# Down projection of four pairs of token tiles as a Strassen product

## The chip, the cores and the metric

The kernel runs on one core of one Trainium2 chip. The metric is the device time of one execution in microseconds (us). The engines are TensorE (PE, its weight loads are shown as PEld), VectorE (DVE), ScalarE (ACT), GpSimd (POOL) and SyncE (SP), which issues all data transfers (DMAs) here. Each engine works through its own queue in order and waits on semaphores of the others.

## The reference

One transformer block on 2048 tokens of width 512, all in float32: pre-norm sliding-window attention (32 heads of 16, window 256) and then a gated layer.

```python
def _B_ref(x, w_gate, w_up, w_down):
    g = jnp.einsum("bsd,df->bsf", x, w_gate)      # 512 -> 1376
    u = jnp.einsum("bsd,df->bsf", x, w_up)
    h = _sigmoid(g) * u
    return jnp.einsum("bsf,fd->bsd", h, w_down)   # 1376 -> 512

x = A_x
h = x + _A_ref(_layernorm(x, axis=-1), A_wqkv, A_wo)
h2 = h + _B_ref(_layernorm(h, axis=-1), B_w_gate, B_w_up, B_w_down)
```

The change concerns the last product, with `w_down`, for 8 of the 16 tiles of 128 tokens.

## The kernel before

**Numbers.** Every float32 operand of a large product is split into a high and a low float16 half, scaled by a power of two, and a product is three matmuls (high by high, high by low, low by high) that add up in one PSUM accumulator. A matmul has a stationary block of up to 128 x 128 (loaded by a weight load) and streams up to 512 columns past it.

**Stages.** Attention fills the time up to about 400 us. Its blocks overlap: projections (`do_qk`, `do_v`), scores for the row maximum (`do_s`), transposed scores and exponentials (`do_st`), weighted values (`do_pv`), output projection (`do_wo`). From there to about 524 us the weights of the gated layer are loaded, scaled and split (`do_split`, `do_T`), the last attention blocks end, and tiles 0 to 3 go through gate and up projection in the plain way (`do_early`, `do_gu`). The last stage, from about 524 us, takes tiles 4 to 15 in six pairs p = 2 to 7 (tiles 2p and 2p + 1).

**The last stage.** `do_pair` normalizes the two tiles of a pair, forms the Strassen combinations of their activations (S1 to S4), splits them into halves and transposes them by DMA into `x7`. `do_group(p, kind)` then computes gate (kind 0), up (kind 1) and the last 352 columns of both (kind 2) with seven products in place of eight: a pair of tiles and two halves of the contraction make a 2 x 2 matrix, two column blocks of the weight another, and the weight combinations T1 to T4 were made once by `do_T`. Its accumulators X, Y, Z lie in three PSUM banks, from the ring `s`, or from `st` and the bank `pvp`. A first product is copied out (p1), later ones add to it. Group numbers in the table are 3(p - 2) + kind.

The result of kind 1, times the sigmoid of kind 0, gives the hidden activations of 512 columns per tile (columns 0 to 511 and 512 to 1023); kind 2 gives the last 352. `row(t, c, ...)` splits each into halves (`hhi`: a cast on ACT or DVE; `hlo`: a subtraction on DVE or POOL), and a DMA on SP's queue transposes it into a buffer `hT`. `do_down(t)` multiplies: 11 steps over the hidden dimension, each of 3 matmuls with 512 output columns, in one bank of the ring `mm`; then one DVE instruction scales and adds the residual, and a DMA stores the tile:

```python
for f in range(NF):                       # NF = 11
    r = min(P, F - f * P)
    mm3(ps, lambda a, f: hT[t, f // 4][0][:r, a, f % 4, :], lambda a, f: W["d", 3][:r, a, f, :], f, NF)
...
V.scalar_tensor_tensor(y, ps, cd, X[:, slot(t), :], op0=ALU.mult, op1=ALU.add)
```

**Order.** Nothing is scheduled at run time. Each piece (`do_down(4)` and so on) is a generator that yields once per step, with a planned cost per engine, what it needs, and buffers from rings that it takes. A search done beforehand found an order of all steps; it stands in the string `TABLE`, as names such as `down4` or `group3.2/a`. `.2` is the third follow-up piece of group 3; `/a`, `/v`, `/g` choose ACT, DVE or POOL where a step can run on several; `*3` repeats. The steps are emitted in that order, so the table fixes the queue of each engine. A down step of one tile can stand anywhere behind its transposes, and the table puts such steps between the groups' products.

Of the kernel before, what the change touches and what calls it, by code (L numbers as in the profile page):

```python
# [50 lines left out]
SU = float(2.0 ** -16)  # L51
# [25 lines left out]
s2.2 qk8 s2 open_work0 s2 qk8 s2.3 qk8 s2.5 s2.4 ln11 s3 qk8 s3 s2 qk8 s3.0 qk8 s3.1 qk8 ln11 prep3/g prep3/a s2.6 s3 s2 qk9 s3.2 qk8/a amax7/a s3 s2.7 s3.3
qk9 s3*2 qk9 s3.4 s3.5 qk9*2 s4 qk8 s3 qk9*2 s3 qk9 s4.0 s3.6 s4 qk10 s3.7 qk9/a prep3/a amax5/a s4 qk10 s4.1 m0 s4 s4.2 s4 qk10*3 s4 qk10 s4.3 s4.4 s4 m0 qk9
s4.5 m0 s4.6 s5 qk10*2 qk11 s4 qk10/a s5.0 qk11 s5 s4.7 qk11 s5 s5.1 s5.2 s5 qk11 s5.3 s5 qk11*2 s5 s5.4 qk10 qk11 s6 s5.5 s6.0 qk11 s5 s6 s5 qk11/a s5.6 st0
s6.1 st0 ln6 s5.7 s6 st0.0 st0.1 qk11 s6.2 ln7/a s6 st0*2 s6*2 st0.2 ln10 ln8 ln7/g st0.3 st0 keys2 keys1 ln6/a s6.4 s6.3 s6.5 s7 s6 amax8/v keys2 st0 s6 v5  # L80
st0.5 s7.0 s6.6 s6.7 st0.6 s7*2 st1 s7.1 ln7 s7.2 st1.0 st0.4 ln9 st0.7 s7*2 ln7/a ln8/v s7.3 s7.4 st1 s7 s7.5 v5 st1 s7*2 st1.1 st1.2 s7.6 s8 st1 s7.7 st1.3
st1 s8 s8.0 st1.5 s8 st1.4 st1 s8.1 v5 pv0 s8*2 queries8 st1.6 s8.2 m1 queries8 ln8/a st2 s8 s8.3 st1.7 st2 v5 m1 st2.0 s8.4 st2.1 ln8/g s9 st2 s8 s8.5 st2
pv0 v5/a st2.2 ln9/a st2.3 s8.6 s9.0 ln12 ln8 m1 s9 pv0/a s8 st2 st2.5 s9 s9.1 s9.2 keys2 qk14 st2 s9 s8.7 qk14 s9.3 st3 qk14 st2.6 ln12 st2.4 st2.7 pv0 qk14
s9*2 st3 st3.0 st3 s9.4 s9 qk14 st3.1 s9.5 st3.2 qk14 ln9/a s9.6 s9 st3*2 s10 s9.7 st3.3 qk14 s10 ln9/g st3.5 s10.0 st3 s10.1 s10 qk14 st3.6 s10.2 st3.4 st4
s10 qk15 s10 s10.3 st4.0 st4 st3.7 fill1 s11 s10.4 st4 st4.1 pv1 qk15 s11 st4 s10 st4.2 ln10/v qk14/a st4 s10.5 s11.0 s11.1 pv1 queries8 ln9 queries9 o0 amax9
queries9*2 st4.3 st4.5 ln13 st4.4 prep3/g st4 s11 pv1/a s11 st5 st4.6 s11.3 s11.2 qk15 s10 qk15 st5.0 qk15 s10.6 pv1 ln10/a st5*2 s10 s11 qk15 st5.1 o1 st5.2
s10.7 s11 st5 st5.3 st5 s11.4 s11 st5.5 st5 s11.5 pv2 s11 queries10 s11.6 st5.6 ln10/g st4.7 st5.4 qk15*2 st6 s12 s11.7 st6.0 qk14 st5.7 s12 st6 s12 st6 m2
qk15/a pv2 s12.0 s12.2 st6.2 ln11/a st6.1 m2 amax10 amax11 m2 queries10 s12.1 st6 s12*2 pv2/a s12.3 st6 s12 st6.3 st6.5 st6 st6.4 s12.4 s12.5 st6.6 s12 s12.6
st7 s13 st7.0 st7 s12 s13.0 pv2 s12.7 queries10 st7.1 st7*2 s13 st7.2 st7.3 st7 s13 s13.1 s13 st7 st7.5 s13.2 s13 s13.3 queries11 st7.6 st8 s13 s13.4
queries11 st8.0 s13.5 queries11 s13 st8 pv3 s14 s13.6 st8.1 st6.7 o0/g st7.7 st7.4 st8 s13 s14 st8 s14.0 qk15 s14.1 s13.7 ln14 pv3 o2 keys3 st8.3 st8.2 s14  # L90
pv3/a st8*2 s14*2 st8.6 s14.2 qk12*2 st8.7 s14.3 s14.4 st9 s15 o1/g st8.4 st8.5 pv3 s15.0 qk12 st9 s14 st9.0 keys3 o3 st9.1 s15 qk12 st9 s14.5 s14 qk12 st9.2
s15.1 st9 s14 st9.3 s14.6 s15 st9 s15 qk13 s14.7 st9.6 st9.4 st9.5 o2/g st9 s15.2 pv4 s15 qk12 st9.7 s15.3 s15 st10 s15.4 qk13 s15 st10.0 s15.5 s16 qk12 st10
s15.6 st10.1 st9.8 st8.8 s16.0 s16 st10 qk12 s15 s16.1 qk13 s16 st10 st10.2 s15.7 s16 st10 s16 pv4 qk12/a o3/v m3 wo1 s16.4 s16.2 qk12 m3 wo1/g st10.3 st10.6
wo1/a s16.3 wo0 m3 pv4/a st10 s17 st11 s16 s17.0 st10.7 qk13 s16 s16.5 qk13 s16 st11.0 s16.6 st11 s17 s16.7 st11 st11.1 s17 s17.1 wo1/g wo1 ln13 wo0/g st10.5
qk13 st11.2 s17.2 s17 st11 s17 s17.3 qk13 st11.3 s17.4 st11 s17*2 st11.6 st11 s17.5 pv5 s17 qk13 s17.6 st11.7 s18 st12 s17.7 s18.0 s18 st12.0 st12 s18 wo1
s18.1 st11.5 st11.4 st10.4 st10.8 st12.1 st12 s18 st12 s18 s18.2 pv4 st12.2 st11.8 s18 wo1 s18.3 st12.3 s18.4 st12 s18 qk13/a st12.6 st12 st12.7 wo0/a st12.5
s18 st12.8 wo0/g keys2 o4 o4/g ln15 s18.5 s18.6 s18.7 amax9/v pv5 qk13 s19 st13 s19 st13 st13.0 s19.0 s19 wo1 queries12 amax12 queries12 queries13 s19.1
st13.1 s19.2 s19 st13 st12.4 pv5/a s19 s19.3 st13 st13.2 s19.4 s19 wo1 s19.5 pv5 st13.3 s19 st13 qk18 s19 st13.6 st13.5 s19.6 s19.7 st13 st13.7 qk18 s20 st14
m4 s20*2 st14.0 s20.0 st13.8 st14 qk18 s20.2 s20.1 st14.1 s20 st13.4 st14 qk18 st14.2 s20.3 st14 pv6 s20*3 st14 pv6 st14.6 amax10/a st14.3 ln14 amax11/v s20.5
s20.4 s20.6 wo1 amax12/v o5 queries14 wo0 m4 amax15 st14 pv6/a s20 st15 s21 queries13 amax14 queries14 s20.7 amax11 st14.7 s21 wo0 s21.0 st15.0 s21.1 st14.5  # L100
# [187 lines left out]
def tile_block(ctx, tc, x, wqkv, wo, wg, wu, wd, out):  # L288
# [944 lines left out]
    def do_down(t):  # L1233
# [7 lines left out]
        for c in range(3):  # L1241
            plan.free(f"hT{c}", hT[t, c][1], e)
# [216 lines left out]
```

## Time and profile before

| | |
|---|---|
| time, median of 3 runs | 770.11 us (770.04 to 770.41) |
| profiled execution, its own time | 769.71 us |
| span of that execution | 768.0 us |
| instructions in the span | 18055 |
| busy: PE, PEld, DVE, ACT, POOL | 739.6, 466.6, 586.5, 429.5, 339.3 us |
| mean granted TensorE clock | 0.999 |

A span runs from the first to the last instruction; an execution's own time is a little longer. Busy times are of one engine each and overlap one another. A busy PE is not PE at its peak, because consecutive matmuls are drawn overlapping; the distance from one matmul to the next is read from the chain that ended last, which adds up runs of them. A group of instructions is shown with its source line, engine, output and inputs, count, busy time, mean duration of one, and the idle time ahead of it on its engine with what ended it.

### The profile page before, as it was taken

Reading aid. Unit: us, or ns where it says so; the run is one execution under the profiler, and the core shown is the slowest. Engines: PE = TensorE matmul, PEld = TensorE weight load, DVE = VectorE, ACT = ScalarE, POOL = GpSimd, SP = SyncE. Lnnn points to the kernel's source line nnn. Section 1 sums busy time; section 2 is a strip of 40 time slices with the busy share of each in tenths; the row PEclk is TensorE's granted clock in tenths of the full one; section 3 lists DMA queues with packets and bytes.
Section 4 is the critical chain, followed back from the end, with each engine's and each line's share of the span. In section 5 each row is a group of like instructions: output and inputs, shape, how many; then the busy total and the mean of one; then the engine's idle time right before and its main releaser. Section 6 shows DMA issues by size and latency. Waiting matters only on the chain.

```text
span 768.0 us, 18055 instructions
## 1 busy us (share of the span) xinstructions
PE 739.6 (96%) x6714; PEld 466.6 (61%) x6714; DVE 586.5 (76%) x1767; ACT 429.5 (56%) x756; POOL 339.3 (44%) x428
## 2 busy tenths in 40 slices
PE   5799999999999999999999799999999999999998
PEld 4577777777787678787665444454544444444453
DVE  6979999887988888688879989976554657566452
ACT  6736888887776787786778866630142122121220
POOL 8732647554444554555556556430341224234210
PEclk9999999999999999999999999999999999999999
DMA  9883563656946626536455768543434433434333
GB/s 332 216 216 107 146 169 69 164 109 128 198 112 163 136 65 147 105 78 135 85 87 140 181 151 236 124 77 72 99 86 93 107 72 96 83 67 101 66 82 83
DMA packets 168567, 95.68 MB, mean 125 GB/s; under 512 B 140640, under 2 KB 146784, under 8 KB 168480
## 3 DMA queue, kind: packets, MB, share of 16 engines
q1 hardware_dynamic: 168480, 94.54, 52.7%
q8 instruction: 52, 0.85, 0.5%
q14 instruction: 35, 0.29, 0.1%
HBM read 35.26 MB, written 13.11 MB: 63 GB/s over the span
## 4 chain that ended last, share of the span: by engine, by line
PE 79%; DVE 12%; issue 4%; POOL 3%; ACT 2%; DMA 1%; DVEq 0%; POOLq 0%; ACTq 0%
PE mmp L358 31%; PE sp L1086 10%; PE pvp L742 9%; PE sp L654 8%; PE stp L1086 7%; PE stp L716 3%; PE pvp L1086 3%; PE stp L706 3%; PE sp L358 2%; PE stp L705 2%; DVE junk L641 2%; PE stp L707 1%; PE stp L358 1%; DVE Tu L985 1%; ACT pa L683 1%
## 5 line engine op out<-in xcount | busy, mean ns | idle before, releaser
L641 DVE CUSTOM_DVE_ANT_0 junk<-sp,mask 128x320 bf16<-128x320 f32 (+4 forms) x512 | 214.8, 465 | 38.1 <-PE sp L654 35.7
L683 ACT ACTIVATE pa<-stp,kappa 128x512 f32<-128x512 f32 (+1 forms) x256 | 156.0, 645 | 36.5 <-PE stp L707 31.0
L654 PE MATMUL sp<-SK,SQ 96*128 96x256 f16 (+3 forms) x960 | 129.2, 232 | 2.3 <-DVE mq L641 1.6
L1086 PEld LDWEIGHTS <-SQ 128*128 128x128 f16 x756 | 73.9, 98 | 75.5
L358 PE MATMUL mmp<-xT,W 128*128 128x256 f16 x768 | 109.5, 273 | 0.5 <-DVE xT L313 0.5
L358 PE MATMUL mmp<-WD,hT 128*128 128x512 f16 (+1 forms) x408 | 98.7, 379 | 0.0
L654 PEld LDWEIGHTS <-SQ 96*128 96x128 f16 x960 | 79.5, 97 | 26.4 <-issue 9.0
L683 ACT ACTIVATE pb<-stp,kappa 128x512 f32<-128x512 f32 x128 | 84.1, 685 | 19.2 <-PE stp L716 17.2
L689 POOL TENSOR_SCALAR_AFFINE_SELECT pa<-pa 128x1024 f32<-128x1024 f32 x56 | 62.2, 1113 | 38.3 <-ACT pa L683 35.1
L358 PEld LDWEIGHTS <-W 128*128 128x128 f16 x768 | 70.2, 97 | 9.8 <-issue 1.0
L358 PEld LDWEIGHTS <-hT 128*128 128x128 f16 (+1 forms) x408 | 39.9, 98 | 45.3
L694 POOL TENSOR_SCALAR_AFFINE_SELECT pa<-pa 128x512 f32<-128x512 f32 x64 | 41.8, 655 | 53.0 <-ACT pa L683 52.9
L742 PE MATMUL pvp<-pa,VT 128*17 128x128 f32 (+1 forms) x1408 | 62.5, 307 | 0.5 <-DVE rh L754 0.5
L694 POOL TENSOR_SCALAR_AFFINE_SELECT pb<-pb 128x512 f32<-128x512 f32 x64 | 42.0, 660 | 44.0 <-ACT pb L683 43.3
L706 PE MATMUL stp<-SQ,SK 100*128 100x256 f16 x224 | 60.0, 271 | 0.0
L707 PE MATMUL stp<-SQ,SK 100*128 100x128 f16 x256 | 55.3, 218 | 0.5 <-ACT pb L683 0.2
L358 PE MATMUL mmp<-WO,oT 128*128 128x512 f16 x192 | 50.4, 378 | 1.9 <-DMA oT<-whl 1.5
L742 PEld LDWEIGHTS pvp<-pa,VT 128*17 128x17 f32 x1408 | 37.8, 97 | 23.4 <-issue 2.8
L705 PE MATMUL stp<-SQ,SK 100*128 100x128 f16 x224 | 49.4, 220 | 2.7 <-ACT pa L683 1.8
L358 PE MATMUL mmp<-W,xT 128*128 128x512 f16 x192 | 49.7, 378 | 1.9 <-DVE sq L580 1.9
L716 PE MATMUL stp<-SQ,SK 100*128 100x256 f16 x256 | 48.3, 272 | 2.5 <-ACT pa L683 2.4
L358 PEld LDWEIGHTS <-x 128*128 128x128 f16 x288 | 28.0, 98 | 28.5 <-issue 1.8
(322 smaller groups left out, 1351.1 us busy)
## 6 DMA issues: line engine op xcount, KB each, us to landing
SQ<-sq SPq DMA_DIRECT2D x96, 128.0 KB
SK<-mem SPq DMA_DIRECT2D x16, 384.0 KB
chunk<-in_wd_dram SPq DMA_DIRECT2D x20, 256.0 KB
mem<-sk SPq DMA_DIRECT2D x8, 512.0 KB
out_dram<-WO SPq DMA_DIRECT2D x16, 256.0 KB
X<-in_x_dram SPq DMA_DIRECT2D x7, 512.0 KB
chunk<-in_wu_dram SPq DMA_DIRECT2D x12, 256.0 KB
xs<-X SPq DMA_DIRECT2D x10, 256.0 KB
```

The costliest lines, as they stand in the source:

```text
L358: PE.matmul(ps, a_of(a, k), b_of(b, k), start=(k == 0 and i == 0), stop=(k == n - 1 and i == 2))
L641: V.tensor_tensor_reduce(out=junk[:, c0:], in0=ps[:, c0:], in1=mask[:, c0:], scale=1.0, scalar=-3.0e38, op0=ALU.add, op1=ALU.max, accum_ou ...
L654: PE.matmul(ps[:, col:col + k1 - k0], q, SK[0:96, (2 * a + hf) % 5, 4 * (p % 2) + j, k0:k1], start=True, stop=True)
L683: S.activation(dst, a, AF.Exp, scale=kappa)
L689: G.affine_select(out=f, in_=f, pattern=[[0, 8], [-1, 128]], compare_op=ALU.is_gt, fill=0.0, base=0, channel_multiplier=1)
L694: G.affine_select(out=p, in_=p, pattern=[[0, 4], [1, 128]], compare_op=ALU.is_ge, fill=0.0, base=0, channel_multiplier=-1)
L705: PE.matmul(a[:, 0:128], ks(k0, g, j), qs(b, g, j, 0, 128), start=True, stop=True)
L706: PE.matmul(a[:, 128:384], ks(k0 + 1, g, j), qs(b, g, j, 0, 256), start=True, stop=True)
L707: PE.matmul(a[:, 384:512], ks(k0 + 3, g, j), qs(b, g, j, 128, 256), start=True, stop=True)
L716: PE.matmul(a[:, u, :], ks(k0 + 2, g, j + u), qs(b, g, j + u, 0, 256), start=True, stop=True)
L742: PE.matmul(ps[32 * j:32 * j + 17, u, q0:q1], VT[:, kt % 6, 8 * j + g, :], w[:, j, c:c + q1 - q0], start=first, stop=last, skip_group_chec ...
L1086: PE.matmul(out, x7[p][0][:, kk, MATS[a], ha, :], mv, start=first and i == 0, stop=i == 5, skip_group_check=True)
```

## The change

For pairs p = 3 to 6 (tiles 6 to 13) the first 1024 of the 1376 hidden columns of the down projection are multiplied by Strassen's algorithm: the two tiles by two blocks of 512 hidden columns, against two blocks of 512 rows of `w_down` by two blocks of 256 output columns. The other 352 hidden columns are multiplied plainly, in the same accumulators, by output halves of 256 columns (`rest`). Tiles 0 to 5, 14 and 15 keep `do_down`.

- `do_sums(k)`, four times: loads two blocks of `w_down` again, makes T1 to T4 with four subtractions (POOL or DVE), and splits each into halves (a cast and a DVE instruction each). They lie in buffers that other weights have left (`retire`), and the loads use the one buffer `FS`, which `do_pair` also uses from p = 3 on, in place of three.
- `do_mat(p, m)`, seven for a pair: the operands A11, A12, A22 and the sums S1 to S4 of hidden activations, each split into halves and transposed by a DMA. They take the place of four `row` pieces.
- `do_mix(p)`: seven products of 12 matmuls and four remainders of 9, all of 256 columns, with accumulators X, Y, Z in three banks and W in one of `mm`; copies and additions of 256 columns on DVE, ACT or POOL; the residual and the scale are applied by the same DVE instructions that combine; then two stores.
- The rings of row and transpose buffers for the first two column blocks become one each (`h` of 4, `hT` of 6). Scale constants change by powers of two.
- Some planned costs change (for example 0.68 in place of 0.8 for a load of x, 1.1 in place of 0.85 for the rows of maxima), and `TABLE` is found anew from its start: 4458 steps in place of 4345, a different order throughout.

```diff
+MIX = range(3, 7)
...
+                if p in MIX:
+                    Aq[p, "A" + q] = a, i
+                    plan.mark(("a", p, "A" + q), e)
+                    return
                 yield from row(t, c, a, e, lambda z: plan.free("E", i, z))
...
+    def do_sums(k):
+        e, nF = yield {DMA_: 0.475}, ["retired", ("scale", "d")], ["FS"], 0.8
...
+        nc.sync.dma_start(f[:, 0], wd[k * P:k * P + P, :])
...
+        nc.sync.dma_start(f[:, 1], wd[512 + k * P:512 + k * P + P, :])
...
+        e, = yield {POOL_: 2.76, DVE_: 1.4}, [e]
+        E = G if plan.on == POOL_ else V
+        for o, x, y in ((a, b, a), (b, d, b), (d, d, a), (c, c, d)):
+            E.tensor_tensor(out=o, in0=x, in1=y, op=ALU.subtract)
+        for m, x in (("T1", a), ("T3", b), ("T2", d), ("T4", c)):
+            e, = yield {ACT_: 0.4, DVE_: 0.25}, [e]
+            copy(TD[m][:, 0, k // 2, k % 2], x, sc["sd"])
+            e, = yield {DVE_: 0.38}, [e]
+            V.scalar_tensor_tensor(TD[m][:, 1, k // 2, k % 2], x, sc["sd"], TD[m][:, 0, k // 2, k % 2], op0=ALU.mult, op1=ALU.subtract)
...
+    def do_mat(p, m):
...
+        add, sub = {DVE_: 0.602, POOL_: 1.113}, ALU.subtract
+        if m == "S1":
+            e, i = yield add, [("a", p, "A21"), ("a", p, "A22")], ["tp"]
+            x = TP[i % RINGS["tp"]]
+            Hm[p, "M"] = x, i
+            tt(x, quad("A21"), quad("A22"), ALU.add)
...
+        e, nh = yield {ACT_: 0.52, DVE_: 0.335}, [e], ["h"]
+        h = hrow["h"][nh % len(hrow["h"])]
+        copy(h[:, 0], x)
+        e, = yield {DVE_: 0.602, POOL_: 1.113}, [e]
+        subtract(h[:, 1], x, h[:, 0])
...
+        e, nt = yield {DMA_: 1.295}, [e], ["hT"], 1.4
...
+    def do_mix(p):
+        rings, bank = (("s",) * 3, None) if p % 2 else (("st", "st", "pv"), pvp[0])
+        n = D // 2
...
+            for c in range(4):
+                for ha, hb in ((0, 0), (0, 1), (1, 0)):
+                    PE.matmul(ps[r][0], x[:, ha, c, :], moving_d(b, hb, c), start=first and k == 0, stop=last and k == 11, skip_group_check=True)
...
+        e = yield from prod("X", "A11", "B11", True, False, rings[0])
+        plan.add(snap("X", "p1", e))
...
+        e = yield from prod("Z", "S1", "T1", True, False, rings[1])
+        plan.add(snap("Z", "z", e))
+        plan.add(w())
+        e = yield from prod("Y", "S2", "T2", True, False, rings[2])
+        plan.add(u2(e))
+        e = yield from rest("W", t1, hi, True, "mm")
+        plan.add(w22(e))
+        yield from prod("X", "A12", "B21", False, False, needs=[(key, "p1")])
+        e = yield from rest("X", t0, lo, False)
+        plan.add(c11(e))
+        e = yield from prod("Y", "S3", "T3", False, True, needs=[(key, "u2")])
+        plan.add(c22(e))
+        yield from prod("Z", "S4", "B22", False, False, needs=[(key, "z")])
+        e = yield from rest("Z", t0, hi, False, free=True)
+        plan.add(c12(e))
+        yield from prod("Y", "A22", "T4", False, False, needs=[(key, "c22")])
+        e = yield from rest("Y", t1, lo, False, free=True)
+        plan.add(c21(e))
```

More of the change, by code (lines that the diff above doesn't have):

```diff
@@ L923, in row @@
         m = PADDED[c]
-        e, nh = yield alt("hhi", ACT_, ACT=n / 1200 + 0.093, DVE=n / 1920 + 0.069), [e], [f"h{c}"]
-        h = hrow[c][nh % len(hrow[c])]
+        rh, rt = ("h2", "hT2") if c == 2 else ("h", "hT")
+        e, nh = yield alt("hhi", ACT_, ACT=n / 1200 + 0.093, DVE=n / 1920 + 0.069), [e], [rh]
+        h = hrow[rh][nh % len(hrow[rh])]
         copy(h[:, 0, :n], a)
@@ new lines, in do_mat, with quad, gone, spare @@
+    def do_mat(p, m):
+        def quad(q):
+            return Aq[p, q][0]
+        def gone(q, n, e):
+            plan.join(("gone", p, q), n, e, lambda z: plan.free("E", Aq.pop((p, q))[1], z))
+        def spare(e):
+            plan.join(("spare", p), 2, e, lambda z: plan.free("tp", Hm.pop((p, "M"))[1], z))
+        def tt(out, x, y, op):
+            (G if plan.on == POOL_ else V).tensor_tensor(out=out, in0=x, in1=y, op=op)
+        add, sub = {DVE_: 0.602, POOL_: 1.113}, ALU.subtract
[4 more added lines that the diff above has]
+            tt(x, quad("A21"), quad("A22"), ALU.add)
+            plan.mark(("sum", p, m), e)
+            gone("A22", 2, e)
+        elif m == "S2":
+            e, = yield add, [("a", p, "A11"), ("mat", p, "S1")]
+            x = Hm[p, "M"][0]
+            tt(x, x, quad("A11"), sub)
+            plan.mark(("sum", p, m), e)
+            gone("A11", 3, e)
+        elif m == "S3":
+            e, = yield add, [("a", p, "A11"), ("a", p, "A21"), ("sum", p, "S1")]
+            x = quad("A21")
+            tt(x, quad("A11"), x, sub)
+            gone("A11", 3, e)
+        elif m == "S4":
+            e, = yield add, [("mat", p, "A12"), ("sum", p, "S2")]
+            x = quad("A12")
+            tt(x, x, Hm[p, "M"][0], sub)
+            spare(e)
+        else:
+            e, = yield {DVE_: 0.0}, [("a", p, m)]
+            x = quad(m)
+        e, nh = yield {ACT_: 0.52, DVE_: 0.335}, [e], ["h"]
[3 more added lines that the diff above has]
+        subtract(h[:, 1], x, h[:, 0])
+        plan.mark(("mat", p, m), e)
+        if m == "A11":
+            gone(m, 3, e)
+        elif m == "A22":
+            gone(m, 2, e)
+        elif m == "S2":
+            spare(e)
+        elif m in ("S3", "S4"):
+            gone({"S3": "A21", "S4": "A12"}[m], 1, e)
+        e, nt = yield {DMA_: 1.295}, [e], ["hT"], 1.4
+        plan.free("h", nh, e)
+        Hm[p, m] = hTs["hT"][nt % len(hTs["hT"])], nt
+        nc.sync.dma_start(Hm[p, m][0].rearrange("p h j q -> p (h j) q"), h.rearrange("p h n -> p (h n)"), transpose=True)
+        plan.mark(("H", p, m), e)
@@ new lines, in do_mix, with moving_d, bank_of, prod @@
+    def do_mix(p):
+        rings, bank = (("s",) * 3, None) if p % 2 else (("st", "st", "pv"), pvp[0])
+        n = D // 2
+        t0, t1 = 2 * p, 2 * p + 1
+        key = ("mix", p)
+        ps, tp, ys = {}, {}, {}
+        dn, lo = 0.337, slice(0, n)
+        hi = slice(n, D)
+        base = [("TD", k) for k in range(4)] + [("W", "d", f, 3) for f in range(NF)]
+        def moving_d(m, h, k):
+            if m in TD:
+                return TD[m][:, h, k // 2, k % 2]
+            return W["d", 3][:, h, k + 4 * (m[1] == "2"), hi if m[2] == "2" else lo]
+        def bank_of(ring, place):
+            t = bank.rearrange("p a x -> p (a x)") if ring == "pv" else psum_tile(ring, [P, 512])
+            return t[:, :n], ring, place
+        def prod(r, a, b, first, last, ring=None, needs=()):
+            e, *place = yield {PE_: 12 * (n / 2400 + 0.0025)}, [("H", p, a)] + base + list(needs), [ring] if ring else []
+            if ring:
+                ps[r] = bank_of(ring, place[0])
+            x, i = Hm.pop((p, a))
+            k = 0
+            for c in range(4):
+                for ha, hb in ((0, 0), (0, 1), (1, 0)):
+                    PE.matmul(ps[r][0], x[:, ha, c, :], moving_d(b, hb, c), start=first and k == 0, stop=last and k == 11, skip_group_check=True)
+                    k += 1
+            plan.free("hT", i, e)
+            return e
+        def rest(r, t, cols, first, ring=None, needs=(), free=False):
+            e, *place = yield {PE_: 9 * (n / 2400 + 0.0025)}, [("h", t, 2)] + base + list(needs), [ring] if ring else []
+            if ring:
+                ps[r] = bank_of(ring, place[0])
+            k = 0
+            for f in range(8, NF):
+                q = min(P, F - f * P)
+                for ha, hb in ((0, 0), (0, 1), (1, 0)):
+                    PE.matmul(ps[r][0], hT[t, 2][0][:q, ha, f - 8, :], W["d", 3][:q, hb, f, cols], start=first and k == 0, stop=k == 8, skip_group_check=True)
+                    k += 1
+            if free:
+                plan.free("hT2", hT[t, 2][1], e)
+            return e
+        def freed(r, e):
+            plan.free(ps[r][1], ps[r][2], e)
+        def snap(r, nm, e):
+            e, i = yield {ACT_: n / 1200 + 0.19, DVE_: dn}, [e], ["tp"]
+            tp[nm] = TP[i % RINGS["tp"]][:, :n], i
+            copy(tp[nm][0], ps[r][0])
+            plan.mark((key, nm), e)
+        def scaled(t, cols, x, base_=None):
+            o = ys[t][0][:, cols]
+            V.scalar_tensor_tensor(o, x, cd, X[:, slot(t), cols] if base_ is None else o, op0=ALU.mult, op1=ALU.add)
+        def done_p1(e):
+            plan.join((key, "p1 read"), 3, e, lambda z: plan.free("tp", tp["p1"][1], z))
+        def half_done(t, e):
+            plan.join(("halves", t), 2, e, lambda z: plan.mark(("y", t), z))
+        def u2(e):
+            e, i = yield {DVE_: dn}, [(key, "p1"), e], ["tp"]
+            o = TP[i % RINGS["tp"]][:, :n]
+            V.tensor_tensor(out=o, in0=ps["Y"][0], in1=tp["p1"][0], op=ALU.add)
+            plan.mark((key, "u2"), e)
+            done_p1(e)
+            e, = yield {DVE_: dn}, [e, (key, "ys")]
+            scaled(t0, hi, o)
+            plan.free("tp", i, e)
+            plan.mark((key, "r12"), e)
+        def w():
+            e, = yield {POOL_: n * 0.00188 + 0.15, DVE_: dn}, [(key, "p1"), (key, "z")]
+            (G if plan.on == POOL_ else V).tensor_tensor(out=tp["z"][0], in0=tp["z"][0], in1=tp["p1"][0], op=ALU.add)
+            plan.mark((key, "w"), e)
+            done_p1(e)
+        def w22(e):
+            e, = yield {DVE_: dn}, [(key, "w"), e]
+            V.tensor_tensor(out=tp["z"][0], in0=ps["W"][0], in1=tp["z"][0], op=ALU.add)
+            freed("W", e)
+            e, = yield {DVE_: dn}, [e, (key, "ys")]
+            scaled(t1, hi, tp["z"][0])
+            plan.free("tp", tp["z"][1], e)
+            plan.mark((key, "r22"), e)
+        def r21():
+            e, = yield {DVE_: dn}, [(key, "p1"), (key, "ys")]
+            scaled(t1, lo, tp["p1"][0])
+            plan.mark((key, "r21"), e)
+            done_p1(e)
+        def c11(e):
+            e, = yield {DVE_: dn}, [e, (key, "ys")]
+            scaled(t0, lo, ps["X"][0])
+            freed("X", e)
+            half_done(t0, e)
+        def c12(e):
+            e, = yield {DVE_: dn}, [e, (key, "r12")]
+            scaled(t0, hi, ps["Z"][0], 1)
+            freed("Z", e)
+            half_done(t0, e)
+        def c22(e):
+            e, = yield {DVE_: dn}, [e, (key, "r22")]
+            scaled(t1, hi, ps["Y"][0], 1)
+            plan.mark((key, "c22"), e)
+            half_done(t1, e)
+        def c21(e):
+            e, = yield {DVE_: dn}, [e, (key, "r21")]
+            scaled(t1, lo, ps["Y"][0], 1)
+            freed("Y", e)
+            half_done(t1, e)
+        def places():
+            for t in (t0, t1):
+                e, i = yield {DVE_: 0.0}, [], ["y"]
+                ys[t] = Y[:, i % RINGS["y"]], i
+            plan.mark((key, "ys"), e)
+        def store(t):
+            e, = yield {DMA_: 0.475}, [("y", t)], [], 0.8
+            plan.free("y", ys[t][1], e)
+            nc.sync.dma_start(out[t * P:(t + 1) * P, :], ys[t][0])
+        e = yield from prod("X", "A11", "B11", True, False, rings[0])
+        plan.add(snap("X", "p1", e))
+        plan.add(places())
+        plan.add(r21())
+        e = yield from prod("Z", "S1", "T1", True, False, rings[1])
[16 more added lines that the diff above has]
+        plan.add(c21(e))
+        for t in (t0, t1):
+            plan.add(store(t))
+        plan.mark(key, e)
@@ L1241, in do_down @@
         for c in range(3):
-            plan.free(f"hT{c}", hT[t, c][1], e)
+            plan.free("hT2" if c == 2 else "hT", hT[t, c][1], e)
         e, place = yield {DVE_: 0.663}, [e], ["y"]
@@ L1339, in later @@
         e, = yield {DMA_: 0.0}, ["p2", ("stash", 12 + c)]
-        plan.free(f"h{c}", 0, e)
+        plan.free("h", c, e)
     def vacant(i):
@@ L1430, in tile_block @@
                 plan.add(do_group(t // 2, kind))
-        plan.add(do_down(t))
+            if t // 2 in MIX:
+                for i, m in enumerate(("A11", "S1", "S2", "A12", "S3", "S4", "A22")):
+                    plan.add(do_mat(t // 2, m))
+                plan.add(do_mix(t // 2))
+        if t // 2 not in MIX:
+            plan.add(do_down(t))
+    for k in range(4):
+        plan.add(do_sums(k))
     with tc.manual_schedule(engines={getattr(mybir.EngineType, e) for e in ("PE", "DVE", "Activation", "Pool", "SP")}):
```

396 lines of the change are left out of this document (208 added, 188 removed).

## Prediction

> **What bounds the kernel now.** I read the page's busy shares and slices first, then busy time by stage, then the chain that ended last, then who waits for whom.
>
> ```profile
> PE 739.6 (96%) x6714; PEld 466.6 (61%) x6714; DVE 586.5 (76%) x1767; ACT 429.5 (56%) x756; POOL 339.3 (44%) x428
> PEclk9999999999999999999999999999999999999999
> 0.00:50.00 50.00, 36.46 (x313) 29.02 (x314) 39.67 (x92) 30.81 (x63) 32.37 (x50) 1.00 0.84 256
> 50.00:400.00 350.00, 346.00 (x4366) 260.09 (x4368) 301.30 (x1210) 268.07 (x471) 181.29 (x238) 1.00 0.56 125
> 400.00:524.00 124.00, 116.91 (x851) 61.27 (x844) 108.63 (x201) 79.78 (x125) 59.95 (x70) 1.00 0.63 150
> 524.00:764.00 240.00, 240.00 (x1191) 116.23 (x1189) 136.14 (x265) 50.81 (x97) 65.70 (x71) 1.00 0.39 84
> ```
>
> Columns of a stage: its window, its length, then busy PE, PEld, DVE, ACT, POOL with counts, granted clock, DMA share, GB/s. From 524 us, where the Strassen groups of the last stage begin, PE is busy 240.00 of 240.00 us at clock 1.00. That alone could hide small stalls, because matmuls are drawn overlapping; the chain excludes it.
>
> ```profile
> 553.40 0.65 PE mmp L358 x3
> 567.10 2.59 PE stp L1086 x12
> 655.65 6.47 PE mmp L358 x30
> 748.68 15.56 PE mmp L358 x72
> 764.24 0.03 issue
> 764.26 0.75 DVE WO L1246
> ```
>
> In 510 to 764 us the chain is PE alone, one matmul after another at the same pace: 30 in 6.47 us, 72 in 15.56 us, 0.216 us each for 512 columns, and the list of waits shows no PE wait there. So a column taken from TensorE in that stage is worth its full price, as long as nothing else becomes late. PE is idle 13.5 us in the first 50, 4.0 in the next 350, 7.1 in 400 to 524 and about 3.8 behind the last matmul. The profiled execution took 769.71 us for a span of 768.0; the median of the runs shown, 770.11, lies 0.4 above it, and I take the sum off the median.
>
> **The PE term.** Tiles 6 to 13 are four pairs. A pair's down projection is now 2 tiles x 11 steps x 3 = 66 matmuls of 512 columns. After, seven products of 12 and four remainders of 9, 120 matmuls of 256 columns: 30,720 columns instead of 33,792, but 54 more instructions and weight loads. The price of 256 columns with a new weight block each time is in the query and key projections, in runs without a gap:
>
> ```profile
> 63.36 0.66 PE mmp L358 x6
> 64.51 0.98 PE mmp L358 x9
> L358 PEld LDWEIGHTS <-W 128*128 128x128 f16 x768 | 70.2, 97 | 9.8 <-issue 1.0 <-DVE sq L580 0.3
> ```
>
> 0.98 / 9 = 0.109 us. A weight load lasts 0.097 and fits under it. So 66 x 0.2157 = 14.24 us go and 120 x 0.109 = 13.08 come, a gain of 1.16 per pair and **4.6 us** in all. The break-even price is 14.24 / 120 = 0.1186 us a matmul; the margin is only a tenth.
>
> [...]
>
> **The other engines.** Prices are from these rows of the last stage, and 256-wide DVE work from the weight sums of the stage before:
>
> ```profile
> L1246 DVE SCALAR_TENSOR_TENSOR WO<-mmp,cd,X 128x512 f32<-128x512 f32 x16 | 12.0, 747 | 18.5 <-PE mmp L358 18.4
> L313 DVE CAST X<-x 128x512 f16<-128x512 f32 x10 | 5.7, 569 | 0.1
> L318 DVE TENSOR_TENSOR X<-x,X 128x512 f16<-128x512 f32 x7 | 5.0, 709 | 0.8 <-ACT X L311 0.7
> L1105 DVE TENSOR_TENSOR x<-stp,chunk 128x512 f32<-128x512 f32 x4 | 2.7, 686 | 4.9 <-PE stp L1086 2.9 <-POOL chunk L1128 2.0
> L1105 DVE TENSOR_TENSOR chunk<-sp,chunk 128x352 f32<-128x352 f32 x6 | 3.0, 514 | 0.0
> L1161 DVE SCALAR_TENSOR_TENSOR X<-WO,X 128x176 f32<-128x176 f32 x6 | 1.9, 334 | 1.6 <-ACT X L1159 1.6
> L978 DVE TENSOR_TENSOR X<-X 128x256 f32<-128x256 f32 x12 | 5.1, 422 | 0.3
> L318 POOL TENSOR_TENSOR X<-x,X 128x512 f16<-128x512 f32 x13 | 15.5, 1196 | 43.9 <-ACT X L311 24.9 <-DVE X L313 18.2 <-ACT x L1135 0.9
> L311 ACT ACTIVATE X<-x 128x512 f16<-128x512 f32 x10 | 6.2, 624 | 11.0 <-DVE x L1144 8.3 <-POOL X L318 2.8
> L933 SPq DMA_TRANSPOSE RT<-X x8: 1232/1240/2012, 566.6 to 744.9; - x8
> ```
>
> Instructions are counted in the two tables by their engine marks. DVE gets: in the 28 transposed operands 22 additions or subtractions of 512 (of 44; POOL has 22) x 0.709 = 15.6 and 7 casts x 0.569 = 4.0; in the four combinations 44 operations of 256 x 0.422 = 18.6; in the weight sums 16 subtractions, 9 casts and 16 low halves x 0.422 = 17.3. It loses 8 outputs x 0.747 = 6.0, and of the 16 rows that had a transpose each 12 casts x 0.569 = 6.8 and 7 subtractions x 0.709 = 5.0. Net +37.7: from 136 to 174 us in a stage of 235, 74%. POOL gets 22 x 1.196 = 26.3 and loses 9 x 1.196 = 10.8, from 66 to about 81; ACT gets 21 casts x 0.624 and about ten pieces of under 0.5, less 4 casts, from 51 to about 66. SP gets 28 transposes for 16, 12 x 1.24 = 15 us more of issue, and eight loads of 256 KB. On the average all of it lies beside PE, and I cost it at nothing there; if the cover went, the dearest part would be DVE's.
>
> New waits in PE's own queue: the products S3, S4, A12 and A22 that add into an accumulator wait until VectorE or ScalarE has read it (one 0.42 operation); everything PE has is queued behind, as in the groups today. On SP, 28 transposes wait for low halves from POOL or DVE; behind them stand the next pair's transposes and the output stores. The output stores have nobody waiting but the reload of X two pairs later; a late transpose stops the product that uses it.
>
> **Where the average does not hold.** I went along the new table, adding DVE work by these rows to PE work by the matmul price. The densest stretch goes from the eighth step of down3 to the third product of mix0: all four weight sums, five of the first operands' additions, the pair normalization and three groups' combinations, 50.7 us of DVE against 44.7 of PE. Single durations overstate, since neighbours overlap: from the first Strassen product on the same count gives 146.7 for the old table, where the trace has 137.0, a factor of 0.93, so 47.1. DVE falls behind by 2.4 us, and by 6.0 at most; at least by nothing, since 22 steps of down4 and down5 stand in that stretch, which need only rows finished in its first two thirds, and mix0 needs the sums but not what DVE does behind them. No row shows such an overload (the densest 20 us of the old table have 16.7), so I take **2.0**, near the worked value. After it no stretch of 20 us has more than 0.96 of PE by the same uncorrected count.
>
> The end: behind the last group product 18 down steps (11.7 us) remain where 24 (15.56) were. The last third of tile 14 is used 8.0 us after its product, of tile 15 9.7. The row chain is addition 0.51, sigmoid, 0.33, cast and subtraction, about 3.2, then 1.24 of issue and a landing that this row bounds:
>
> ```profile
> 370.43 4.73 DMA oT<-whl
> ```
>
> That makes at most 9.2 against 8.0 and 9.7: between 0 and 1 us, taken as 0, as the 4.73 contains queueing behind other transfers. The last output and its store stay as they are.
>
> **The table before 524 us** is also found anew, with the same instructions. Engine marks differ in few places; the one with a price is the subtractions for the weight combinations T3 to T6 of the table, which go from POOL to DVE: 16 x 0.422 = 6.8 us into 400 to 524, where DVE is busy 108.6 of 124.
>
> ```profile
> L978 POOL TENSOR_TENSOR F<-F 128x256 f32<-128x256 f32 x12 | 11.9, 998 | 3.8 <-issue 3.3
> 420.00:430.00 10.00, 8.05 (x101) 4.75 (x101) 9.79 (x18) 9.75 (x16) 3.04 (x3) 1.00 0.88 177
> 430.00:440.00 10.00, 7.77 (x100) 4.58 (x98) 9.86 (x16) 8.32 (x14) 8.05 (x9) 1.00 0.88 215
> 470.00:480.00 10.00, 10.00 (x48) 4.49 (x46) 9.93 (x17) 4.85 (x7) 5.89 (x6) 1.00 0.89 269
> ```
>
> Against it, each subtraction is 0.58 us shorter than on POOL, so a set of four ends 2.3 us earlier. Bounds: a gain of the 7.1 us of PE idle there, a loss of 6.8; I take 0, as 15.4 us of DVE are free. The first 400 us I cost at nothing between -3 and +3: 17.5 us of PE idle that a new order could shift either way.
>
> Sum: 770.1 - 4.6 + 2.0 + 0 + 0 = **767.5 us**.
>
> **Rivals.** (1) The new table has no stall and wins back some early PE idle: for it speaks that 24 us of idle lie ahead of 524; against, that DVE has no room in 420 to 440. 770.1 - 4.6 - 1.5 = 764. (2) DVE's overload falls on PE nearly whole, or mats hold the five activation buffers so long that the next pair's groups wait: with 4 to 6 us back, 770. For it speaks a DVE share of 74% where it was 57; against, those 22 down steps beside the densest stretch. (3) Slower: the T subtractions now on DVE push the start of the last stage. Place 400 to 524, price up to 6.8; it decides from 4.6 - 2.0 + 1.5 = 4.1 us on. 770.1 + 2.2 to 4.2, about 773. For it speak the two stretches with DVE at 9.8 of 10; against, 15.4 us free and the shorter sets. (4) The halved matmuls do not keep half the price, so the change doesn't do what it says: weight loads exposed, 0.109 + 0.097 a matmul, 24.7 us a pair, 812 us. The 0.98 for nine speaks against it. [...]
>
> **The numbers.** What can be told from no change is 0.2%, 1.5 us. Forecast 0.48, its own range 766 to 769; rival 1 0.14; rival 2 0.18; rival 3 0.17; rival 4 0.03. Faster takes most of the forecast (0.45) and rival 1: 0.59; within 0.2% rival 2 and 0.03: 0.21; slower 0.20. The range takes in rival 1 with half of the 400-to-524 idle, 762, and rival 3 at 773; beyond it I leave rival 4 and some 0.05 on each side.
>
> **What would show it.** Right: down matmuls of 256 columns at 0.109 us in the chain; PE busy about 236 from the first group on; DVE there near 174; a PE wait of 1 to 3 us on DVE or a transpose around the first combination. Wrong: PE waits spread over all four combinations, a first group product later or earlier than 524 by over 2 us, or a matmul price over 0.1186.

## The result, and the profile after

The median went from 770.26 us (770.04 to 771.13) to **765.58 us** (765.22 to 765.89). The ratio is 0.9937, with an interval of 0.992 to 0.9954: faster by 0.5 to 0.8%. The profiled execution took 765.89 us for a span of 764.0, 4.0 us less than the span before.

The page's busy shares and clock of the kernel after, then its busy time by stage with the columns of the prediction:

```profile
PE 734.1 (96%) x6930; PEld 486.5 (64%) x6930; DVE 630.1 (82%) x1887; ACT 442.8 (58%) x770; POOL 337.6 (44%) x418
PEclk9999999999999999999999999999999999999999
0.00:50.00 50.00, 37.40 (x328) 30.16 (x329) 40.92 (x98) 30.16 (x58) 32.81 (x52) 1.00 0.84 267
50.00:400.00 350.00, 346.26 (x4384) 260.42 (x4382) 301.86 (x1216) 268.29 (x469) 183.13 (x240) 1.00 0.61 125
400.00:524.00 124.00, 117.61 (x835) 60.74 (x834) 108.11 (x214) 76.67 (x121) 42.94 (x51) 1.00 0.62 148
519.53:764.00 244.47, 237.33 (x1410) 137.20 (x1408) 181.63 (x367) 67.71 (x123) 78.72 (x76) 1.00 0.54 107
```

And pieces of the chain that ended last, after:

```profile
514.99 4.54 PE mmp L363 x21
519.53 3.88 PE sp L1095 x18
...
547.56 4.55 PE mmp L363 x21
...
575.04 0.48 DVE F L1274
...
582.06 3.86 DMA hT<-X
...
599.27 0.41 DVE WO L1408
...
602.65 5.39 DMA RT<-X
608.09 1.48 PE sp L1367 x12
...
650.20 1.31 PE stp L1367 x12
...
748.55 11.67 PE mmp L363 x54
760.22 0.03 issue
```

The start of the last stage in the same view of the kernel before:

```profile
519.38 4.54 PE mmp L358 x21
523.92 1.29 PE sp L1086 x6
```

(L1095 after is L1086 before, the group products; L1367 is the new 256-column product; L363 after is L358 before.) Three things are to be read here.

First, the last stage begins 4.4 us earlier: 519.53 against 523.92. The kernel after has done 30 down steps of three matmuls ahead of it where the kernel before had done 31, so 0.65 us of that is work put off, and 3.7 are gained.

Second, the last stage is no shorter. By the trace's matmul starts it runs from 519.36 to 759.83 us, 240.5 us from the first group product to the last matmul, and before from 523.76 to 763.85, 240.1 us (the chain counts the same pieces from 0.16 us later). With the 0.65 in it, its own work gained 0.2 to 0.3 us. The rest of the 4.0 us came from the part that the change was not about. Stage lengths below are taken in the same way.

Third, the chain in that stage was PE alone before. After, it leaves PE between 552 and 608 us for VectorE and transfers, and after that it is PE again.

So the 256-column matmuls cost what was forecast, 12 in 1.31 us, 0.109 each, and their 4.6 us went into stops. I added up the distance from each matmul start to the next beyond the price of one (0.216 us for 512 columns, 0.109 for 256), from the trace: 4.43 us in the last stage after, 0.18 before. The stops end at 592.1 (1.51 us), 597.9 (0.28), 601.7 (0.61), 606.2 (1.24) and 608.1 (0.52), and a few are under 0.1. The list of PE's waits in the last stage, after:

```profile
PE sp L1367 <- DMA RT<-X: 1.4, 2, 1.1
PE stp L1095 <- DVE X L1114: 1.3, 1, 1.3
PE mmp L1380 <- DMA hT<-X: 0.4, 1, 0.4
```

Columns: us in total, times, longest. One wait is for VectorE: an addition of group 5 (L1114) has to read the accumulator before the group's last product adds to it. Three are for transposes of the first combination's operands; the two named RT hold S3 and S4, for the fifth and sixth product. The list adds up to 3.1 us, the starts to 4.4: a matmul is drawn some 0.16 us beyond its place in the stream, and what passes between release and start is in no wait, so each stop is worth more than the list shows. Busy time by stretch around it, after:

```profile
547.00:572.00 25.00, 25.00 (x121) 11.71 (x120) 23.91 (x50) 9.39 (x19) 7.43 (x7) 1.00 0.59 136
572.00:592.00 20.00, 18.75 (x97) 9.29 (x95) 19.24 (x47) 5.80 (x11) 1.59 (x1) 1.00 0.70 147
592.00:608.00 16.00, 13.98 (x102) 9.62 (x101) 12.62 (x33) 4.39 (x9) 5.84 (x6) 1.00 0.88 157
```

VectorE is full for 45 us (43.15 of 45), beside an idle POOL (1.59 of 20); then PE stops. The DMA engines have their densest share of this stage, 0.88, while PE waits for transposes.

### The profile page after: what moved, and what is told of

Same layout as the page of the kernel before. It is cut to its first block, busy times and chain, and to the rows that moved or that the text cites. A ratio compares the mean times of both kernels' runs of the same rounds, so it can differ in the third digit from the quotient of the medians.

```text
span 764.0 us, 18698 instructions
## 1 busy us (share of the span) xinstructions
PE 734.1 (96%) x6930; PEld 486.5 (64%) x6930; DVE 630.1 (82%) x1887; ACT 442.8 (58%) x770; POOL 337.6 (44%) x418
## 4 chain that ended last, share of the span: by engine, by line
PE 73%; DVE 12%; DMA 7%; ACT 4%; issue 3%; SPq 1%; DVEq 0%; ACTq 0%
PE mmp L363 23%; PE pvp L747 9%; PE sp L1095 8%; PE sp L659 8%; PE stp L1095 5%; PE stp L721 3%; PE stp L711 3%; PE stp L363 2%; PE pvp L1095 2%; PE sp L1367 2%; PE stp L710 2%; PE stp L712 2%; PE stp L1367 1%; PE sp L363 1%; DVE junk L646 1%
## 5 line engine op out<-in xcount | busy, mean ns | idle before, releaser
L659 PE MATMUL sp<-SK,SQ 96*128 96x256 f16 (+3 forms) x960 | 127.6, 232 | 2.9 <-DMA SK<-mem 1.2
L1095 PEld LDWEIGHTS <-SQ 128*128 128x128 f16 x756 | 73.8, 98 | 73.0 <-issue 1.6
L363 PE MATMUL mmp<-xT,W 128*128 128x256 f16 x768 | 109.8, 272 | 1.8 <-ACT xT L316 1.6
L363 PEld LDWEIGHTS <-W 128*128 128x128 f16 x768 | 70.0, 97 | 12.5 <-issue 4.1
L363 PE MATMUL mmp<-WO,oT 128*128 128x512 f16 x192 | 50.6, 379 | 0.9 <-DMA oT<-whl 0.9
L363 PE MATMUL mmp<-W,xT 128*128 128x512 f16 x192 | 49.5, 379 | 0.0
L363 PE MATMUL mmp<-WD,hT 128*128 128x512 f16 (+1 forms) x204 | 48.6, 379 | 0.0
L363 PEld LDWEIGHTS <-x 128*128 128x128 f16 x288 | 27.9, 98 | 28.7 <-issue 1.8
L646 DVE DVE_READ_ACCUMULATOR2_ANT mq<- 128x1 f32 x512 | 42.5, 83 | 0.0
```

The lines of the kernel that those rows point to most:

```text
L363: PE.matmul(ps, a_of(a, k), b_of(b, k), start=(k == 0 and i == 0), stop=(k == n - 1 and i == 2))
L646: V.tensor_tensor_reduce(out=junk[:, c0:], in0=ps[:, c0:], in1=mask[:, c0:], scale=1.0, scalar=-3.0e38, op0=ALU.add, op1=ALU.max, accum_ou ...
L659: PE.matmul(ps[:, col:col + k1 - k0], q, SK[0:96, (2 * a + hf) % 5, 4 * (p % 2) + j, k0:k1], start=True, stop=True)
L1095: PE.matmul(out, x7[p][0][:, kk, MATS[a], ha, :], mv, start=first and i == 0, stop=i == 5, skip_group_check=True)
```

## Experiments

Four theories. **A**: the gain in time comes from the new order of the steps ahead of the last stage. **B** (the prediction's): it comes from the last stage. **C**: the 4.4 us of stops come from VectorE, which the weight sums overload. **D**: they come from SP's queue, with 28 transposes for 16 and eight loads.

**A against B.** The kernel before, with the steps ahead of the first group product in the new table's order and the rest in the old one's; three steps in it run as soon as a buffer is free.

```diff
 # kernel before
 TABLE = """
-load_x0 load_w0 load_x1 load_w1 load_w2 load_w3 zeros0 load_x3 ln0 load_x2 load_w4 load_w13
...
+load_x0 load_x1 load_w1 load_w2 load_w0 load_w3 zeros0 ln0 load_w14 load_x3 load_w9 load_w8
...
```

> Kernel before (no Strassen in the down projection), but every step ahead of the first group product in the order of the changed kernel's table, the rest in the old order (three steps that find no free row buffer run as soon as one is free). Theory A, from the two traces: the first group product starts 4.4 us earlier in the changed kernel (519.5 against 523.9 us) with 0.65 us less down work done, so the new order of the first part alone is worth 3.75 us and the Strassen part nothing: 766.5 us. Theory B, as the prediction had it: the front is worth 0 and the last stage 2.6: 770 us.

Measured: 766.85 us against 769.96, ratio 0.9963 (0.9949 to 0.9977). Its chain at the start of the last stage:

```profile
515.14 5.83 PE mmp L388 x27
520.97 1.29 PE sp L1116 x6
```

The stage starts 2.95 us earlier than in the kernel before and then takes the 240.1 us that it took there. With no part of the Strassen down products in it, this kernel has 2.8 us (1.8 to 3.9, by the interval) of the change's 4.9 (3.5 to 6.2). Theory A holds. What is missing to the start at 519.53 is 1.44 us: 0.65 for the down step, and 0.7 that it is already late at its long run of projections, which starts at 27.05 us where the kernel after has 26.36. The last section has the likely cause.

**The opposite half.** The changed code with the old order ahead of the first group and the new one behind it. The new code's buffers allow the old order only with 15 steps put off, gate, up and down steps among them.

```diff
 # kernel after
 TABLE = """
-load_x0 load_x1 load_w1 load_w2 load_w0 load_w3 zeros0 ln0 load_w14 load_x3 load_w9 load_w8
...
+load_x0 load_w0 load_x1 load_w1 load_w2 load_w3 zeros0 load_x3 ln0 load_x2 load_w4 load_w13
...
```

> Changed kernel, but every step ahead of the first group product in the old order, the rest in the order of the new table (15 steps that find no free buffer run as soon as one is free, among them three down and some gate and up steps of TensorE). Theory A: last stage as long as before, 770 us, up to 772 if the late steps cost something. Theory B: 767.5 us.

Measured: 774.68 us, ratio 1.0056 (1.0042 to 1.007), a miss for both theories, because the front lost 5 us: the first group product comes at 529.01. By the matmul starts some 4 of them are lost after 510 us.

```profile
521.54 2.71 DMA hT<-X
524.25 0.05 issue
524.30 4.71 PE mmp L394 x21
529.01 3.88 PE sp L1126 x18
```

The chain shows one of the waits there, for a transpose that nothing covers any more. That the steps put off are the cause is the nearest reading; it was not tried by itself. As a time the run therefore says nothing on A. As a stage it does: from the first group product to the last matmul it took 240.2 us, with 4.8 us of stops, 3.9 of them ending at 601 to 617. The new last stage is no faster behind the old front either.

**C against D: VectorE's share taken away.** The 16 subtractions of the weight sums go from DVE to POOL and 9 of their casts from DVE to ACT; the order of the steps stays.

```diff
 # TABLE of the kernel after: marks of the do_sums steps only
-sums0/v  sums1/v  sums2/v  sums3/v      (subtractions)
+sums0/g  sums1/g  sums2/g  sums3/g
-sums0/v  sums1/v*2  sums2/v*3  sums3/v*3  (casts)
+sums0/a  sums1/a*2  sums2/a*3  sums3/a*3
```

> Changed kernel, the four weight sums' 16 subtractions from VectorE to GpSimd and their 9 casts from VectorE to ScalarE; order unchanged. Theory C, VectorE's overload before the first combination is the stall: 16 x 0.42 + 9 x 0.35 = 9.9 us leave VectorE in 547 to 595 us, the 4.2 us of gaps on TensorE at 592 to 608 us go, 761.5 to 762.5 us. Theory D, the transposes behind SP's queue are (the waits are named after DMA for 1.8 of 3.1 us): a set of subtractions takes 4.2 us on GpSimd in place of 1.8, the one buffer of the sums is held longer, SP's queue with it, and the time is 765.6 to 768 us.

Measured: 763.56 us (762.93 to 764.17), ratio 0.9911 (0.9897 to 0.9926), between the two forecasts. Its PE waits in the last stage, the dense stretch, and the chain at the stop that is left:

```profile
PE sp L1364 <- DMA RT<-X: 1.0, 1, 1.0
PE mmp L1377 <- DMA hT<-X: 0.3, 1, 0.3
```

```profile
572.00:592.00 20.00, 20.00 (x110) 10.60 (x109) 17.27 (x34) 9.41 (x19) 7.90 (x8) 1.00 0.62 135
```

```profile
597.34 1.22 SPq L936
...
598.65 4.99 DMA RT<-X
603.64 0.05 issue
603.69 2.79 PE sp L1364 x24
```

VectorE has 17.27 of 20 instead of 19.24, its wait is gone, and the stage takes 237.8 us; the stops add up to 1.83. So 2.6 of the 4.4 us went with VectorE's load. The rest has another cause, and the chain names it: two transposes stand ahead in SP's queue from 596 us, 1.2 to 1.3 us of issue each, and the one of S3 (RT), for the fifth product of the first combination, follows and lands 4.99 us after the start of its issue.

Moving the casts alone tells how much of the overload it takes:

```diff
 # TABLE of the kernel after
-sums0/v  sums1/v*2  sums2/v*3  sums3/v*3  (casts)
+sums0/a  sums1/a*2  sums2/a*3  sums3/a*3
```

> Changed kernel, only the 9 casts of the weight sums from VectorE to ScalarE, 3.1 us of VectorE time. Theory C: the stall of 4.2 us shrinks by up to 3.1 us, 762.5 to 764 us. Theory D: no change, 765.6 us.

Measured: 764.45 us (762.87 to 765.41), ratio 0.9923 (0.9909 to 0.9937); just over C's forecast by the median; a stage of 238.4 us with 2.43 of stops. Nine casts of 0.28 us each in the chain of the kernel after, 2.5 us in all, give back 2.0 us of stops: four fifths of what was taken from the full VectorE came back on PE here.

**C, the other way.** The 16 low halves of the sums are issued twice, which adds work to DVE in the dense stretch and nothing to any other engine or queue: 16 x 0.42 = 6.7 us by the price of the expectation, 7.7 by the 0.48 us that one takes in this run's chain.

```diff
             V.scalar_tensor_tensor(TD[m][:, 1, k // 2, k % 2], x, sc["sd"], TD[m][:, 0, k // 2, k % 2], op0=ALU.mult, op1=ALU.subtract)
+            V.scalar_tensor_tensor(TD[m][:, 1, k // 2, k % 2], x, sc["sd"], TD[m][:, 0, k // 2, k % 2], op0=ALU.mult, op1=ALU.subtract)
```

> Changed kernel, each of the 16 VectorE instructions that make the low halves of the weight sums issued twice: 16 x 0.42 = 6.7 us more VectorE work in 547 to 590 us, nothing else. Theory C (VectorE is the bound there): nearly all of it reaches TensorE, 770.5 to 772.3 us. Theory D (transposes and SP's queue): VectorE has room, 765.6 to 767 us.

Measured: 774.23 us against 770.55, ratio 1.0048 (1.0035 to 1.0061). PE's waits in the last stage:

```profile
PE stp L1095 <- DVE X L1114: 4.3, 1, 4.3
PE stp L1095 <- DVE x L1114: 2.5, 1, 2.5
```

Both stops are now at the folds of a group, as C has it, and they sum to 7.1 us by the starts, all stops of the stage to 7.6. The time is over what either theory gave. In the profiled execution, one of 775.66 us, the stage takes 248.3 us, 7.9 more than in the kernel after: 3.2 are longer stops, and 4.6 are matmuls at half clock behind the two stops (last section). How much of the added work would have come through at full clock can't be told from this run.

**D's loads.** Six of the eight loads of the weight sums are left out. So that the values stay finite, the subtractions become maxima and the scale a small constant, with as many instructions as before; the kernel leaves out the right sums.

```diff
-        nc.sync.dma_start(f[:, 0], wd[k * P:k * P + P, :])
+        if k == 0:
+            nc.sync.dma_start(f[:, 0], wd[k * P:k * P + P, :])
...
-            E.tensor_tensor(out=o, in0=x, in1=y, op=ALU.subtract)
+            E.tensor_tensor(out=o, in0=x, in1=y, op=ALU.max)
...
-            copy(TD[m][:, 0, k // 2, k % 2], x, sc["sd"])
+            copy(TD[m][:, 0, k // 2, k % 2], x, 1.0e-9)
...
```

> Changed kernel, the loads of the second to fourth weight sum left out (six of eight transfers of 256 KB), subtraction replaced by maximum and the scale by a small constant so that the values stay finite; VectorE's instructions are as many and as long as before. It leaves out the right weight sums. Theory C: no change, 765.6 us within 0.5. Theory D: SP and the DMA engines are relieved and the stall shrinks, 762 to 764 us.

Measured: 765.14 us (763.0 to 767.87), ratio 0.993 (0.9914 to 0.9947), as the kernel after; the stage takes 239.9 us with 3.88 of stops, and DVE is as full:

```profile
572.00:592.00 20.00, 19.94 (x104) 10.01 (x103) 19.32 (x49) 5.86 (x11) 2.23 (x3) 1.00 0.44 89
```

The DMA share of that stretch falls from 0.70 to 0.44 and the stops by 0.55: the loads are at most a small part of the cause.

**The weight sums left out whole**, loads, subtractions, casts and low halves. The products that would use them read plain blocks of `w_down`.

> Changed kernel without the weight sums' loads, subtractions, casts and low halves; the products that would use them read plain blocks of the down weight. It leaves the weight sums out. Theory C: 17 us leave VectorE, the gaps on TensorE at 592 to 602 us go and what is left is the wait for the third and fourth operand's transposes, about 1 us: 761 to 762.5 us. Theory D: 763.5 us or more, as the operands' transposes stay.

Measured: 763.76 us (762.39 to 764.19), ratio 0.9908 (0.9896 to 0.9921). Waits of PE, and the dense stretch:

```profile
PE sp L1364 <- DMA RT<-X: 0.7, 1, 0.7
PE mmp L1377 <- DMA hT<-X: 0.6, 1, 0.6
PE stp L1095 <- DMA SQ<-OS: 0.5, 1, 0.5
```

```profile
572.00:592.00 20.00, 20.00 (x108) 10.46 (x107) 12.16 (x24) 5.72 (x10) 3.97 (x3) 1.00 0.38 76
```

No wait for VectorE is left, with 12.16 of 20. Yet 2.5 us of stops are, all three on transposes (SQ is of the next pair's activations). C had expected all but about 1 us to go and is wrong by the rest. VectorE and the transposes share the 4.4 us: by this run 1.9 to 2.5, by the sums off DVE 2.6 to 1.8.

**A version from this.** The kernel with the sums off DVE has its largest stop, 1.12 us, at the fifth product of the first combination. One PE step, the fourth product of group 7, is moved ahead of it, to cover the transpose.

```diff
 # TABLE of the kernel with the sums off DVE
-... pair3 mix0 mat5 mat6 ... group6 group7 group6.4 ...
+... pair3 group7 mix0 mat5 mat6 ... group6 group6.4 ...
```

> The kernel with the weight sums' subtractions on GpSimd and casts on ScalarE (763.56 us), and the fourth product of group 7 moved ahead of the first combination's seventh step, which waited 1.1 us there for two transposes that SP had issued back to back. If that wait is only a matter of the order, the 1.29 us product covers it: 762.4 us. If moving the product only moves a wait elsewhere: 763.6 us.

Measured: 763.24 us (762.42 to 764.48), ratio 0.9906 (0.9893 to 0.9919). In the trace the wait for RT is gone and one is left:

```profile
PE mmp L1377 <- DMA hT<-X: 0.5, 1, 0.5
```

```profile
592.00:608.00 16.00, 15.53 (x115) 10.87 (x113) 12.29 (x33) 3.88 (x7) 5.26 (x6) 1.00 0.81 153
```

The last stage takes 236.9 us with 0.86 of stops: 240.1 - 4.6 + 0.65, and 0.86 of stops where the kernel before had 0.18, make 236.8, so the account of that stage closes. In the times it can't be told from the version without the move (763.56); both are faster than the kernel before, by 0.7 to 1.1%, and by their ratios (0.9911 and 0.9906 against 0.9937) some 0.3% ahead of the kernel after.

## Why the prediction was right or wrong

The time came out 1.9 us under the forecast: inside the whole range of 762 to 773, just under the forecast's own of 766 to 769, and by other terms than those it added up. That the sum came so near is luck: a stall of 4.4 where 2.0 stood and a gain of 3.7 where 0 stood cancel in part.

- **The PE term, -4.6: right.** 12 in 1.31 us is the 0.109 that nine projections in 0.98 us had given, with a new weight block each time and at 54 more instructions a pair. Rival 4, with 0.206 a matmul, falls.
- **The stall, +2.0: right in place, right in cause for about half, and too small.** It came where the densest stretch was worked out, between the eighth step of down3 and the first combination, and the sums filled VectorE. It measured 4.4, inside the bounds of 0 to 6. (For the kernel before the working names 16.7 us of DVE in the densest 20; its trace has at most 15.7 in the last stage, which changes nothing in the argument.) The working had corrected the count of DVE work by 0.93 to an overload of 2.4 and shaved that to 2.0; what VectorE really costs is 1.9 to 2.6. The larger omission is the 1.8 to 2.5 us of transposes: the prediction named them as a possible wait ("a late transpose stops the product that uses it") and gave them no price. It had 1.24 us of issue and up to 4.73 of landing in its own rows, and in the kernel after three in a row, the third that of the fifth product, made more than the cover there: the product stopped for 1.24 us, up to 606.2.
- **The table before 524 us, 0: wrong, and the step that failed.** "I take 0", with bounds of -7.1 to +6.8 and of another 3 either way, for an order that is new throughout. It measured -3.7. The prediction treated it as noise around the old order because no instruction was added. The bound held, the value did not, and it was as large as the term the change was made for. The prediction had named the sign that would refute it, a first group product over 2 us away from 524, and that is what came. Where the new order wins can be read only in part. The weighted values, by line and first and last start in the kernel before and after:

```profile
L742 PE MATMUL pvp<-pa,VT x1408: 271/273/393, 85.9 to 447.5; 128*17 128x128 f32 x120, 128*17 128x256 f32 x56
```

```profile
L747 PE MATMUL pvp<-pa,VT x1408: 271/273/393, 83.6 to 443.3; 128*17 128x128 f32 x120, 128*17 128x256 f32 x56
```

  These 1408 matmuls begin 2.3 us earlier and end 4.2 us earlier. So by 84 us over half is there, and nearly all by 443. Adding up each matmul's place in the stream says the same: 20 us of work are done at 38.1 us before and at 35.7 after, a lead of 2.3 that stays at about 2 to 3 up to 420 us, and the rest comes between 420 and 448. The first part is where the kernel before has PE idle for 1.88 of the 5 us from 30 on, shown here before and after:

```profile
30.00:35.00 5.00, 3.12 (x28) 2.54 (x26) 4.85 (x10) 4.23 (x8) 4.57 (x5) 1.00 0.79 169
30.00:35.00 5.00, 5.00 (x40) 3.38 (x38) 4.65 (x10) 2.90 (x5) 4.84 (x7) 1.00 0.57 187
```

  PE's drawn idle time shows less of it: over 0 to 524 us PE is busy 501.3 us instead of 499.4. Which of the moved steps give it was not tried one by one and stays open.
- **The end, 0: right.** 54 matmuls stand behind the last group product, 11.67 us, without a stop, as forecast.
- **Other engines.** PE is busy 237.3 us from the first group on (forecast 236), POOL 78.7 (81), ACT 67.7 (66). DVE has 181.6 where 174 was forecast: 100 instructions more than before in the last stage instead of 87. The nine casts of the sums, priced at 0.422 each, took 0.28 in the chain.
- **Rivals.** Rival 1 had won-back idle time ahead of 524, and half of its mechanism came, but its "no stall" did not. Rival 2's 4 to 6 us of stops came, at 4.4, and its 770 did not, since the front paid for them. Rival 3, the slower one, is wrong in sign: the stage starts earlier, and in 400 to 524 us DVE is busy 108.1 us as before (108.6) although POOL gave up 17 us there (59.95 to 42.94).

## What to carry to other kernels

When a schedule is found anew, its unchanged part is an edit of its own: read what limits that part and give it a value with a sign, or say that the forecast can't be better than that part's idle time. Price an engine's overload in the densest stretch, not by its average share, and add the queue that is next in line: when VectorE was relieved, three transposes in a row on SP were already waiting to stop the same products (1.83 us of stops were left). A stop on PE is measured from matmul start to matmul start, because the list of waits showed 3.1 of 4.4 us.

## What the hardware showed that was not expected

**Two long stops of PE cost 4.6 us beyond their length.** In the kernel with the low halves issued twice, busy time and clock around its two stops (the last three columns: granted clock, DMA share, GB/s):

```profile
569.50:572.90 3.40, 0.92 (x5) 0.35 (x4) 3.26 (x8) 0.17 (x1) 0.00 (x0) 1.00 0.31 77
572.90:576.30 3.40, 3.40 (x9) 1.22 (x8) 3.29 (x6) 1.80 (x3) 2.12 (x2) 0.50 0.98 243
...
596.00:600.00 4.00, 0.81 (x6) 0.39 (x5) 3.79 (x11) 0.00 (x0) 0.00 (x0) 1.00 0.85 179
600.00:601.00 1.00, 0.00 (x0) 0.00 (x0) 1.00 (x5) 0.29 (x1) 0.00 (x0) 0.60 0.00 0
601.00:605.00 4.00, 3.88 (x17) 2.34 (x17) 3.16 (x6) 2.68 (x6) 2.44 (x2) 0.50 0.27 51
...
607.00:608.00 1.00, 1.00 (x11) 0.87 (x10) 0.29 (x1) 0.00 (x0) 0.00 (x0) 0.98 0.64 195
```

and the chain behind the second:

```profile
601.12 1.92 PE stp L1095 x6
603.04 4.65 PE sp L1368 x24
```

PE stops for 2.65 us up to 572.75, and the clock is at half from 572.9 to 576.3. It stops for 4.5 us up to 601.12; the clock falls to half about 3.5 us into the stop and stays there until 607.0. By the matmul starts, the matmuls behind the first stop take 1.7 us more than at full clock and those behind the second 2.9 more: six group products of 352 columns take 1.71 us instead of 0.89, and 256 columns 0.21 each instead of 0.109. The half clock lasted 3.4 us behind the first stop, with matmuls in all of them; at the second it lasted 6.8 us, 0.9 of them still in the stop. The 3.4 us ahead of 572.9 held 0.92 us of matmuls as drawn. The stops in the last stage of the kernel after, 1.5 us at most, left its clock at 1.00 there.

A lower clock is also seen at the start of a run, in the kernel before with the new front:

```profile
15.00:20.00 5.00, 4.96 (x31) 3.81 (x31) 4.05 (x13) 3.96 (x10) 2.65 (x7) 0.66 1.05 388
```

The kernel after has 1.00 in these 5 us with the same order of steps. In the 5 us ahead of it PE was busy for 2.80 us, and in the kernel after for 4.04. The one execution lost part of its clock and the other did not, which fits the 0.7 us by which this profile came late to its projections. It is part of the spread of this kernel's times (765.04 to 769.41) at most: of its eleven executions the five with a mean clock of 1.000 took 765.04 to 768.28, median 765.87, and the six with less 766.77 to 769.41; only the profiled one shows its clock in that stretch.

The half clock also came without a long stop. In two profiles, the low halves twice and the loads left out (mean granted clock 0.991 and 0.997), the clock is at half from 412 to 415.5 us, though no matmul there starts over 1.3 us after the one ahead of it, and their last stages start 1.7 and 1.2 us later than that of the kernel after. What sets off such a fall is not shown: no run was made to test it.
